# Moving VectorE sums of the last batch between small products, and sums of T1 beside the last product of batch 1

## The chip, the cores and the metric

One core of a Trainium2 chip. The metric is the device time of one execution in microseconds (us). The span in a profile is the time from its first to its last instruction; in these runs it is about 2 us shorter than the time. Only one core runs. TensorE is PE in the views, VectorE is DVE, ScalarE is ACT.

## The reference

```python
# x: 8 batches x 8 heads x 512 x 64, state: 8 x 8 x 32 x 64
a = softmax(scale * x @ state.T);   xread = a @ state       # 512 rows a batch
a2 = softmax(scale * state @ x.T);  sread = a2 @ x          # 32 rows a batch
y = concat(xread, sread)  ->  (8 * 544, 512)                # heads side by side
h = y @ w_in               # 512 x 2048
g = h * sigmoid(1.702 * h)
out = g @ w_out            # 2048 x 512
```

## The kernel before

All is fp32. From batch 1 on, the last product (g @ w_out) of a batch is done in Strassen's way, which needs seven block products in place of eight and some sums besides. They are called P1 to P7, in the order P1, P2, P5, P6, P3, P7, P4. P1, P2 and P3 are plain: 16 matmuls with an output of 128x256, each of which stands as two records in these traces (48 records of L706 for the 24 matmuls of P1's second half and P2 in the last batch). P5, P6, P7 and P4 are split once more into seven small products of 128x128 each. In batch 1, P5 and P4 are still plain. After batch 7, the last one, a final part takes the 256 rows of sread ("sr"), with sums of w_in that VectorE has to have ready by then. T1 to T4 are sums of blocks of w_out.

TensorE does the products; VectorE forms the sums that go into them and adds the results out of PSUM, the buffer (in banks) that the matmuls of this kernel write to. A sum that nobody needs soon can stand in the program in front of an add for which TensorE waits, and in these traces VectorE ran them in the program's order: in the last batch before, TensorE's last record of P2 ended at 644.76 us, but the add that reads P2's bank started at 650.98, behind the eight half sums ahead of it. `hook("P5.4")` means: what is listed under this name is put here, after the fourth small product of P5.

```python
        product(bank(0), A_of(0, 0), B11, "P1")      # hooks "P1a", "P1b" after its two halves
        nc.scalar.copy(k1, bank(0))
        sums_of(S2, q1, q2, q4)
        if not plain:
            ...
            sums_of(S1, *r)
            third_of(S1)
        product(bank(1), A_of(0, 1), B21, "P2")      # hooks "P2a", "P2b"
        osb = opool.tile([P, 2, HN], FP32, tag="osb", name=f"osb_{key}_00")
        tt(osb, bank(1), k1)                         # reads P2's PSUM bank
        ...
            o, h0, h1 = low_banks()                  # o is bank 1 once more
            strassen_low(left_of(S1, *r), (b11, t3, b21, b22, *low5), [h0, h1, o], p5, at)   # P5

    def strassen_low(left, right, bank, R, at):      # cut to its first products
        product(o[0], a11, b11); nc.scalar.copy(p, o[0]);  at(1)
        product(o[1], s2, t2);   add(u2, o[1], p);         at(2)
        product(o[2], a12, b21); add(c11, o[2], p);        at(3)   # o[2] is P2's bank
        product(o[0], a21, t3);  add(u3, o[0], u2);        at(4)
        ...
```

For the last batch the twenty half sums of w_in (`steps`) are handed out like this:

```python
            order = [("P1b", 2), ("P2a", 8)]
            order += [(name, 1) for name in ("P5.4", "P5.6", "P6.1", ..., "P7.4")]
```

And in batch 1 the three sums of T1 are made at the hook S4, just ahead of P6, into spare buffers, and stored to DRAM:

```python
    def low5_make():
        rooms = spare_M()
        for fn, args in low_sums(T1, [v.rearrange("p (f n) -> p f n", f=QF) for v in rooms[:3]]):
            fn(*args)
        for k in range(3):
            nc.sync.dma_start(outside[5][:, FC * k : FC * (k + 1)], rooms[k])
```

Of the kernel before, what the change touches and what calls it, by code (L numbers as in the profile page):

```python
# [20 lines left out]
def kernel(  # L21
# [30 lines left out]
    nc = tc.nc  # L52

    B, H, S, D = x.shape
# [9 lines left out]
    FC = 512  # L64
# [37 lines left out]
    T1, T2, T4 = (sums[:, i].rearrange("p (f n) -> p f n", f=HF) for i in range(3))  # L102
# [25 lines left out]
    def load_state(b):  # L128
        stn[b] = apool.tile([P, NG, D], FP32, tag="stn", name=f"stn_{b}", bufs=2)
        for g in range(NG):  # L130
            nc.sync.dma_start(stn[b][:, g], st_v[b, g])
# [44 lines left out]
    for i, v in enumerate((8.0 * most, 8.0 * (most - least))):  # L176
        t = konst.tile([P, 1], FP32, name=f"edge_{i}")
# [332 lines left out]
    def quarters(key, u, ntok):  # L510

        g, half = G[key, u], ntok // 2
        return g[:, :, :half], g[:, :, half:ntok]

    def s12(key, u, ntok):

        half = ntok // 2
        (a11, a21), (_, a22) = quarters(key, u, ntok), quarters(key, HF // 2 + u, ntok)
        s1, s2 = S1[:, 2 * u : 2 * u + 2, :half], S2[:, 2 * u : 2 * u + 2, :half]
        nc.vector.tensor_tensor(out=s1, in0=a21, in1=a22, op=ALU.add)  # L520
        nc.vector.tensor_tensor(out=s2, in0=s1, in1=a11, op=ALU.subtract)

    def s3(key, u, ntok):

        a11, a21 = quarters(key, u, ntok)
        nc.vector.tensor_tensor(out=a21, in0=a11, in1=a21, op=ALU.subtract)
# [61 lines left out]
    QF = HF // 2  # L588
    T3 = w_out[:, :HF, HN:]
# [4 lines left out]
    low5 = low3  # L594
    outside = {k: dram.tile([P, 3 * FC], FP32, name=f"low_{k}") for k in (3, 4, 5)}
    turn_room = low[:, 3:].rearrange("p k n -> p (k n)")

    def low_load(k):
        nc.sync.dma_start(turn_room, outside[k])
# [21 lines left out]
    def spare_M():  # L621

        m = [mpool.tile([P, NG, FC], FP32, tag=f"M{i}", name="spare_M") for i in (2, 3)]
        return [v[:, g] for v in m for g in range(NG)]

    def low5_make():
        rooms = spare_M()
        for fn, args in low_sums(T1, [v.rearrange("p (f n) -> p f n", f=QF) for v in rooms[:3]]):
            fn(*args)
        for k in range(3):  # L630
            nc.sync.dma_start(outside[5][:, FC * k : FC * (k + 1)], rooms[k])

    def halves_of(t):

        return [t[:, QF * i : QF * (i + 1), P * k : P * (k + 1)] for i in range(2) for k in range(2)]

    def low_sums(t, rooms):

        b11, b12, b21, b22 = halves_of(t)
        t1, t2, t4 = rooms  # L640
        return [(T_of, v) for v in ((t1, b12, b11), (t2, b22, t1), (t4, b21, t2))]

    def low_third(t):
        _, b12, _, b22 = halves_of(t)
        T_of(b12, b22, b12)
# [39 lines left out]
    def strassen_two(key, dst, hooks, a4):  # L685


        plain = a4 is None
# [7 lines left out]
        def hook(name):  # L696
            for fn, args in hooks.get(name, ()):
                fn(*args)
# [121 lines left out]
        b11, t3, b21, b22 = halves_of(T3)  # L820
        o, h0, h1 = low_banks()
        strassen_low(left3, (b11, t3, b21, b22, *low3), [h0, h1, o], k3, lambda i: hook(f"P7.{i}"))
        if key + 1 < B:
            low_load(5)
        hook("P7")
        osb = opool.tile([P, 2, HN], FP32, tag="osb", name=f"osb_{key}_11")
# [118 lines left out]
    def parts_x(b):  # L945

        a = A[b]
        t1, t2, t3, t4 = ([t] for t in a["T"])
        r11, r21, r22 = [a["aT"][:, 0, :QT]], [a["aT"][:, 1, :QT]], [a["aT"][:, 1, QT:]]

        def left(u):
            c = u // 2
            lo, hi = a["M", c], a["M", 2 + c]
            return [lo[:, 0]], [lo[:, 1]], [hi[:, 0]], [hi[:, 1]], [a["S1"][:, c]], [a["S2"][:, c]], [a["S4"][:, c]]

        return left, (r11, r21, r22, t1, t2, t3, t4)
# [40 lines left out]
    def up_strassen(b, ntok, left, right):  # L997

        QT = ntok // 2
        b11, b21, b22, t1, t2, t3, t4 = right  # L1000
        banks = {}

        def product(u, bank, lhs, rhs, first):
            if first:
                if bank == "x":
                    banks[bank, u] = psH.tile([P, 2, QT], FP32, tag="h", name=f"upx_{b}_{u}")
                else:
                    o = bank_o[2 * (u % 2) + (bank == "z")]
                    banks[bank, u] = o[:, : 2 * QT].rearrange("p (k t) -> p k t", k=2)
            ps = banks[bank, u]  # L1010
            n = len(lhs)
            for k in range(2):
                o = 2 * P * (u % 2) + P * k
                for i in range(n):
                    nc.tensor.matmul(  # L1015
                        ps[:, k], lhs[i][:, o : o + P], rhs[i],
                        start=(first and k == 0 and i == 0), stop=(i == n - 1), skip_group_check=True,
                    )
            return ps

        def gelu(dst, src):
            nc.scalar.activation(out=dst, in_=src, func=AF.Gelu_apprx_sigmoid)  # L1022

        def add(ps, x, dst):
            nc.vector.tensor_tensor(out=dst, in0=ps, in1=x, op=ALU.add)  # L1025


        def begin(u):
            l11, l12, l21, l22, m1, m2, m4 = left(u)
            G[b, u], G[b, NU + u] = free.pop(0), free.pop(0)  # L1030
            _, c12 = quarters(b, u, ntok)
            c21, _ = quarters(b, NU + u, ntok)
            nc.scalar.copy(c21, product(u, "x", l11, b11, True))  # L1033
            add(product(u, "y", m2, t2, True), c21, c12)

        def middle(u):
            l11, l12, l21, l22, m1, m2, m4 = left(u)
            c11, c12 = quarters(b, u, ntok)
            c21, c22 = quarters(b, NU + u, ntok)
            z = product(u, "z", m1, t1, True)  # L1040
            gelu(c11, product(u, "x", l12, b21, False))
            add(product(u, "y", l21, t3, False), c21, c22)
            add(z, c22, c22)
            gelu(c22, c22)

        def end(u):
            l11, l12, l21, l22, m1, m2, m4 = left(u)
            c11, c12 = quarters(b, u, ntok)
            c21, c22 = quarters(b, NU + u, ntok)
            add(product(u, "y", l22, t4, False), c21, c21)  # L1050
            gelu(c21, c21)
            add(product(u, "z", m4, b22, False), c12, c12)
            gelu(c12, c12)
            if u:
                s12(b, u - 1, ntok)

        for u in range(NU):
            begin(u)
            if u:
                end(u - 1)  # L1060
            middle(u)

        def rest():
            end(NU - 1)
            s12(b, NU - 1, ntok)
            for u in range(NU):
                s3(b, u, ntok)

        return rest
# [86 lines left out]
    def T_of(t, x0, x1):  # L1156
        nc.vector.tensor_tensor(out=t, in0=x0, in1=x1, op=ALU.subtract)
# [34 lines left out]
    def out_of(b):  # L1192
        return lambda r, n: out_x[b, r, :, n].rearrange("r q n -> q r n")

    for b in range(1, B):
        if b > 1:
            ahead = {"P1a": [(up_strassen(b, S, *parts_x(b)), ())]}
        else:
            ahead = {
                "P1a": low_sums(T2, low2) + [(T_of, (T4, B21, T2)), (low_third, (T2,))],  # L1200
                "P1b": low_sums(T3, low3) + [(low_keep, (3, turn_room)), (low_third, (T3,))],
                "S4": [(low5_make, ())],
                "P7.5": [(low_third, (T1,))],
            }
        if b + 1 < B:
            hooks = hooks_next(b + 1)
        else:

            steps, left, right = sr_sums()
            order = [("P1b", 2), ("P2a", 8)]  # L1210
            order += [(name, 1) for name in ("P5.4", "P5.6", "P6.1", "P6.3", "P6.4", "P6.6", "P7.1", "P7.2", "P7.3", "P7.4")]
            hooks = {}
            for name, n in order:
                hooks[name], steps = steps[:n], steps[n:]
            assert not steps
            for name, t in (("P6.2", T1), ("P6", T2), ("P4.1", T3), ("P4.7", T4)):
                hooks[name] = [(low_third, (t,))]
        for name, first in ahead.items():
            hooks[name] = first + hooks.get(name, [])
        a4 = {}  # L1220
        k = 3 if b + 1 < B else 0
        hooks.setdefault("P3a", [])[k:k] = [(low4_load if b > 1 else low4_make, (a4,))]
        strassen_two(b, out_of(b), hooks, a4 if b > 1 else None)
        if b == 1:
            low_third(T4)
        if b + 2 < B:
            load_state(b + 2)
            load_x(b + 2)
# [35 lines left out]
```

## Time and profile before

| what | value |
|---|---|
| time | 741.96 us, median of three runs, 741.14 to 742.05 |
| the one execution with a profile | 740.57 us, span 738.7 us |
| TensorE busy | 97% of the span |
| its longest two waits | 5.2 us in the last batch, 1.6 us in batch 1 |
| one batch in the middle | 78.8 us |

The prediction shows the lines of the two waits. Two more readings carry its sums. The first is batch 6, where nothing stands in front of osb, in the timeline of the kernel before (start, us, engine, line, operation, count):

```profile
570.57 1.05 PE L656 MATMUL low<-sums,later 128*128 128x128 f32 x8
...
571.55 0.68 DVE L713 TENSOR_TENSOR osb<-o,g 128x512 f32<-128x512 f32 x1
...
572.36 1.09 PE L656 MATMUL o<-sums,later 128*128 128x128 f32 x8
...
576.85 1.06 PE L656 MATMUL low<-sums,later 128*128 128x128 f32 x8
```

The first and the last of these are the first small products of P5 and of P6: 6.28 us apart, with osb done before the third product is due. The second reading is free time of VectorE in the last batch, during the first half of P1:

```profile
633.58 0.69 DVE L1025 TENSOR_TENSOR g<-o,g 128x512 f32<-128x512 f32 x1 [2.90 <-PE o L1015]
```

VectorE stood idle for 2.90 us there until TensorE released it.

### The profile page before, as it was taken

What the parts mean: (1) busy time and instruction counts of PE and PEld (TensorE: products, weight loads), DVE (VectorE), ACT (ScalarE), POOL (GpSimd) and SP (SyncE); (2) the same over time, 40 slices, a digit from 0 to 9 for tenths busy, and PEclk for the clock granted to TensorE, in tenths of its full rate; (3) what the DMA queues carried; (4) which work ended last, traced back from release to release, by engine and by line L of the source; (5) the groups of instructions that cost most, each with busy time, mean ns of one, the idle gap of its engine ahead of it and who ended that gap; (6) DMA issues with size and microseconds to landing.
All of it is one profiled execution on the core that took longest, in us unless ns stands there. A gap on an engine that the chain in (4) does not pass through costs nothing.

```text
span 738.7 us, 11929 instructions
## 1 busy us (share of the span) xinstructions
PE 719.8 (97%) x4903; PEld 570.6 (77%) x4903; DVE 566.5 (77%) x1156; ACT 235.5 (32%) x436; POOL 0.8 (0%) x8
## 2 busy tenths in 40 slices
PE   8999999999999999999999999999999999979996
PEld 3333444477888889879888889888987898879995
DVE  6997999739866997689867985799669976788440
ACT  4786411033224511432144323442245114200220
POOL 0000000000000000000000000000000000000000
PEclk9999999999999999999999999999999999999999
DMA  9821244011150022201330115002400220020000
GB/s 235 341 96 48 99 158 118 0 58 69 75 146 1 13 88 91 57 1 58 114 76 1 58 47 144 1 17 85 136 12 1 77 108 3 1 101 30 15 1 28
DMA packets 52086, 51.88 MB, mean 70 GB/s; under 512 B 36800, under 2 KB 44480, under 8 KB 52032
## 3 DMA queue, kind: packets, MB, share of 16 engines
q1 hardware_dynamic: 52032, 51.13, 22.2%
q8 instruction: 38, 0.62, 0.3%
q14 instruction: 16, 0.13, 0.1%
HBM read 39.85 MB, written 11.27 MB: 69 GB/s over the span
## 4 chain that ended last, share of the span: by engine, by line
PE 90%; DVE 5%; ACT 2%; DMA 2%; issue 1%; SPq 0%; DVEq 0%; ACTq 0%
PE o L706 19%; PE o L1015 16%; PE low L656 14%; PE o L497 7%; PE o L656 7%; PE h L479 7%; PE upx L1015 6%; PE M L303 4%; PE o L540 2%; PE xT L282 2%; PE o L303 1%; PE sr L459 1%; PE warm L123 1%; PE upx_sr L1015 1%; DMA out_dram<-osb_sr 1%; DVE g L713 1%
## 5 line engine op out<-in xcount | busy, mean ns | idle before, releaser
L1025 DVE TENSOR_TENSOR g<-o,g 128x512 f32<-128x512 f32 (+1 forms) x140 | 88.1, 650 | 85.4 <-PE o L1015 84.5
L706 PE MATMUL o<-w_out,g 128*128 128x256 f32 x672 | 152.7, 381 | 0.0
L706 PEld LDWEIGHTS o<-w_out,g 128*128 128x128 f32 x672 | 125.2, 190 | 26.2 <-issue 10.5
L1022 ACT ACTIVATE g<-g 128x512 f32<-128x512 f32 (+1 forms) x84 | 49.8, 599 | 100.5 <-DVE g L1025 100.5
L1015 PE MATMUL upx<-aT,M 128*128 128x256 f32 x192 | 49.3, 379 | 0.0
L1015 PE MATMUL o<-ta,M 128*128 128x256 f32 x192 | 49.3, 379 | 0.0
L1015 PE MATMUL o<-ta,ms 128*128 128x256 f32 x192 | 48.3, 379 | 0.0
L439 ACT COPY M<-M 128x512 f32<-128x512 f32 x64 | 33.2, 596 | 37.7 <-PE M L303 37.7
L1015 PEld LDWEIGHTS o<-ta,M 128*128 128x128 f32 x192 | 36.5, 190 | 5.0
L1015 PEld LDWEIGHTS o<-ta,ms 128*128 128x128 f32 x192 | 36.5, 190 | 5.0
L1015 PEld LDWEIGHTS upx<-aT,M 128*128 128x128 f32 x192 | 36.1, 190 | 4.7
L656 PE MATMUL low<-sums,later 128*128 128x128 f32 x264 | 34.6, 279 | 0.0
L520 DVE TENSOR_TENSOR later<-g,g 128x512 f32<-128x512 f32 (+1 forms) x32 | 20.8, 649 | 17.6 <-ACT g L482 17.6
L656 PEld LDWEIGHTS low<-sums,later 128*128 128x128 f32 x264 | 33.0, 196 | 0.4
L303 PE MATMUL M<-w_in,stT 64*32 64x512 f32 x512 | 32.7, 594 | 0.2 <-ACT eT L449 0.2
L479 PE MATMUL h<-low,M 128*128 128x512 f32 x64 | 29.8, 600 | 1.4 <-DVE low L388 1.4
L479 PE MATMUL h<-aT,M 128*128 128x512 f32 x64 | 28.7, 599 | 1.4 <-ACT M L439 1.4
L497 PE MATMUL o<-w_out,g 128*128 128x512 f32 x64 | 28.7, 594 | 0.0
L497 PE MATMUL o<-w_out,sums 128*128 128x512 f32 x64 | 28.4, 594 | 0.0
L1033 ACT COPY g<-upx 128x512 f32<-128x512 f32 x24 | 13.7, 572 | 42.4 <-PE upx L1015 42.4
L482 ACT ACTIVATE g<-h 128x512 f32<-128x512 f32 x24 | 14.0, 592 | 40.5 <-PE h L479 40.5
L479 PEld LDWEIGHTS h<-aT,M 128*128 128x128 f32 x64 | 11.8, 190 | 18.3 <-issue 12.2
(200 smaller groups left out, 1262.8 us busy)
## 6 DMA issues: line engine op xcount, KB each, us to landing
low<-low SPq DMA_DIRECT2D x20, 768.0 KB
later<-in_moe_w_out_dram SPq DMA_DIRECT2D x16, 512.0 KB
xn<-in_x_dram SPq DMA_DIRECT2D x28, 256.0 KB
w_out<-in_moe_w_in_dram SPq DMA_DIRECT2D x12, 512.0 KB
out_dram<-osb SPq DMA_DIRECT2D x18, 256.0 KB
out_dram<-later SPq DMA_DIRECT2D x14, 256.0 KB
later<-in_moe_w_in_dram SPq DMA_DIRECT2D x4, 512.0 KB
sums<-in_x_dram SPq DMA_DIRECT2D x4, 256.0 KB
```

The source lines that it names most:

```text
L282: nc.tensor.transpose(ps[:, c], x_heads(b, c, j), ident)
L303: nc.tensor.matmul(ps[g][st], A[b]["stT"][rows, st], rhs(rows, j), start=True, stop=True)
L439: nc.scalar.copy(m[:, g], ps[g])
L479: nc.tensor.matmul(hps, lhs[i], rhs[i], start=(i == 0), stop=(i == n - 1))
L497: nc.tensor.matmul(ops, G[key, f // 2][:, f % 2, P * r : P * (r + 1)], w_out[:, f], start=(f == 0), stop=(f == NF - 1))
L520: nc.vector.tensor_tensor(out=s1, in0=a21, in1=a22, op=ALU.add)
L540: nc.tensor.matmul(ps[:, r], lhs[f][:, P * r : P * (r + 1)], rhs[:, f], start=(first and r == 0 and f == 0), stop=(f == HF - 1), skip_grou ...
L656: nc.tensor.matmul(ps, lhs[f], rhs[:, f], start=(f == 0), stop=(f == QF - 1))
L706: nc.tensor.matmul(ps[:, r], lhs[f][:, P * r : P * (r + 1)], rhs[:, f], start=(r == 0 and f == 0), stop=(f == HF - 1), skip_group_check=True,)
L1015: nc.tensor.matmul(ps[:, k], lhs[i][:, o : o + P], rhs[i], start=(first and k == 0 and i == 0), stop=(i == n - 1), skip_group_check=True,)
L1022: nc.scalar.activation(out=dst, in_=src, func=AF.Gelu_apprx_sigmoid)
L1025: nc.vector.tensor_tensor(out=dst, in0=ps, in1=x, op=ALU.add)
```

## The change

Its intent is to take both waits from TensorE by giving VectorE the same sums in another order. In the last batch four half sums go to the idle time in P1, the other sixteen one by one (twice two small ones together) between small products (one of them beside P3), and none stays between P1 and osb. In batch 1 the sums of T1 move beside the plain P4, and go straight to the buffer where batch 2 reads them. Cut to its core:

```diff
-    def low5_make():
-        ...
-        if key + 1 < B:
+        if not plain and key + 1 < B:
             low_load(5)
@@ batches
+            if b == 2:
+                ahead["P7.5"] = [(low_third, (T4,))]
...
-                "S4": [(low5_make, ())],
-                "P7.5": [(low_third, (T1,))],
+                "P4.7": low_sums(T1, low5) + [(low_keep, (5, turn_room)), (low_third, (T1,))],
@@ the last batch
-            order = [("P1b", 2), ("P2a", 8)]
-            order += [(name, 1) for name in ("P5.4", "P5.6", "P6.1", ..., "P7.4")]
-            ...
-            for name, t in (("P6.2", T1), ("P6", T2), ("P4.1", T3), ("P4.7", T4)):
-                hooks[name] = [(low_third, (t,))]
+            order = (
+                ("P5.4", 2), ("P5.6", 3), ("P6.1", 6), ("P6.3", 7), ("P6.4", 8), ("P6.6", 9), ("P3a", 10), ("P7.1", 11),
+                ("P7.2", 16, 17), ("P7.3", 18, 19), ("P7.4", 12), ("P7.6", 13), ("P4.4", 14), ("P4.6", 15),
+            )
+            hooks = {name: [steps[i] for i in n] for name, *n in order}
+            hooks["P6.2"] = [(low_third, (T1,))]
+            hooks["P4.7"] = [(low_third, (t,)) for t in (T2, T3, T4)]
+            ahead["P1a"][:0] = [steps[i] for i in (0, 1, 4, 5)]
...
-        if b == 1:
-            low_third(T4)
```

More of the change, by code (lines that the diff above doesn't have):

```diff
@@ L624, in spare_M @@
         return [v[:, g] for v in m for g in range(NG)]
-    def low5_make():
-        rooms = spare_M()
-        for fn, args in low_sums(T1, [v.rearrange("p (f n) -> p f n", f=QF) for v in rooms[:3]]):
-            fn(*args)
-        for k in range(3):
-            nc.sync.dma_start(outside[5][:, FC * k : FC * (k + 1)], rooms[k])
     def halves_of(t):
@@ L1209 @@
             steps, left, right = sr_sums()
-            order = [("P1b", 2), ("P2a", 8)]
-            order += [(name, 1) for name in ("P5.4", "P5.6", "P6.1", "P6.3", "P6.4", "P6.6", "P7.1", "P7.2", "P7.3", "P7.4")]
-            hooks = {}
-            for name, n in order:
-                hooks[name], steps = steps[:n], steps[n:]
-            assert not steps
-            for name, t in (("P6.2", T1), ("P6", T2), ("P4.1", T3), ("P4.7", T4)):
-                hooks[name] = [(low_third, (t,))]
+            order = (
[6 more added lines that the diff above has]
+            ahead["P1a"][:0] = [steps[i] for i in (0, 1, 4, 5)]
         for name, first in ahead.items():
```

## The prediction

> **What bounds the kernel now.** I read the page first, then the list of who waited for whom on TensorE, then the timeline around each wait, and last the same stretch of an undisturbed batch.
>
> ```profile
> span 738.7 us, 11929 instructions
> ...
> PE 719.8 (97%) x4903; PEld 570.6 (77%) x4903; DVE 566.5 (77%) x1156; ACT 235.5 (32%) x436; POOL 0.8 (0%) x8
> ...
> PE   8999999999999999999999999999999999979996
> ...
> DVE  6997999739866997689867985799669976788440
> ```
>
> TensorE (PE) is busy 97% of the span, so the end is set by PE's own work plus the few places where PE stands still. After the opening only the 36th slice is below 9, near 650 us, and the last ones. A slice is 18.5 us and hides short holes, so the list of waits comes next (releaser, us in total, times, longest).
>
> ```profile
> PE o L656 <- DVE osb L713: 5.2, 1, 5.2
> PE o L656 <- DVE pu L659: 1.6, 1, 1.6
> PE h L479 <- DVE low L388: 1.4, 1, 1.4
> ```
>
> The two longest happen once each, both in L656 (the small 128x128 products), both for VectorE (DVE). The third lies in the opening, which the change leaves alone. The timeline places the 5.2 us in the last batch, inside P5, between its second and third small product (start, us, engine, line, what, count, idle before):
>
> ```profile
> 645.49 1.06 PE L656 MATMUL low<-low,spare_M 128*128 128x128 f32 x8
> ...
> 646.16 1.28 DVE L975 TENSOR_TENSOR ws<-ws,w_in 128x512 f32<-128x512 f32 x2
> 647.37 1.28 DVE L975 TENSOR_TENSOR w_in<-w_in,w_in 128x512 f32<-128x512 f32 x2
> 648.57 1.28 DVE L975 TENSOR_TENSOR ws<-w_in,ws 128x512 f32<-128x512 f32 x2
> 649.77 1.28 DVE L975 TENSOR_TENSOR ws<-w_in 128x512 f32<-128x512 f32 x2
> 650.98 0.68 DVE L713 TENSOR_TENSOR osb<-o,g 128x512 f32<-128x512 f32 x1
> ...
> 651.71 1.98 PE L656 MATMUL o<-sums,later 128*128 128x128 f32 x8 [5.17 <-DVE osb L713]
> ```
>
> The third product writes the PSUM bank that P2 filled, and that bank is free only when DVE has read it (osb). In DVE's order eight half sums of w_in (L975) stand in front. And after the hole that product took 1.98 us where its neighbours take 1.06. In batch 1 the same picture is smaller: three sums of T1 (spare_M, L1157) and a row sum stand ahead of the add (pu) that frees a bank.
>
> ```profile
> 182.58 0.68 DVE L1157 TENSOR_TENSOR spare_M<-sums 128x512 f32<-128x512 f32 x1
> ...
> 183.30 1.42 DVE L1157 TENSOR_TENSOR spare_M<-sums,spare_M 128x512 f32<-128x512 f32 x2
> 184.63 0.68 DVE L410 TENSOR_REDUCE sm<-e 128x16 f32<-128x512 f32 x1
> 185.23 0.28 DVE L659 TENSOR_TENSOR pu<-o,pu 128x128 f32<-128x128 f32 x1
> ...
> 185.56 1.16 PE L656 MATMUL o<-low,g 128*128 128x128 f32 x8 [1.60 <-DVE pu L659]
> ```
>
> [...]in the window 651.7 to 655.2 us, just after the 5.17 us hole, the granted clock is 0.52, and in 180.2 to 185.5 us, around the 1.60 us hole, it is 1.00. So the first hole costs more than its length and the second does not. [...] The trace shows PE starting at 651.71, 0.05 us after osb ended at 651.66.[...]
>
> **The change part by part.** All durations are rows of the trace before. A 128x512 sum of DVE lasts 0.68 us, but the next starts 0.60 us after it where it doesn't depend on it; one that depends starts 0.72 after.
>
> (1) Last batch, P1 to P2. Ten half sums leave this stretch (two after the quarter sums, eight ahead of osb), some 10 x 0.60 = 6.0 us. Four go to the first half of P1, ahead of the rest of the up product. There DVE is idle 2.90 us (630.68 to 633.58, waiting for PE); four take 4 x 0.60 plus 0.08 for the one that depends, about 2.5 us, so they end near 633.2 and delay nothing. Then the chain runs as before but two sums (1.2 us) shorter: the last sum ahead of osb, which ended at 646.24, ends at 645.0; P2 is done on PE near 644.8 (its last product starts its successor at 644.60). So osb runs 645.0 to 645.7. The third product of P5 is due at 644.60 + 2 x 0.89 = 646.38. The margin is 0.7 us, and PE doesn't wait.
>
> What that is worth: P5's first product to P6's first took 644.60 to 657.91 = 13.31 us. The same stretch of batch 6, with no hole, took 570.57 to 576.85 = 6.28 us. Saved: 7.0 us, of which 5.2 us are the hole and the rest (1.8) the slow clock after it: products three and four took 1.78 and 1.71 us from start to start in place of 0.89 each.
>
> (2) Where the six others of those ten and the rest go: one half sum after a small product. A product takes PE 0.89 us; DVE needs 0.20 for the add and 0.60 for the sum, 0.80, as the old P6 already shows with no wait of PE. The densest is P7: two sums ahead of its first add, then two pairs of 128x256 sums (0.34 each), then two more. From the second product to the fourth DVE needs about 0.2 + 0.7 per 0.89 us. PE looks at a bank again three products later, so a lag of some tenths is covered. Cost: 0.
>
> (3) End of P4: three "third" sums (T2, T3, T4) now stand together ahead of the last sum and of the first add of the final up product; before it was one. That is 2 x 0.60 = 1.2 us later. That add began at 685.63 after 0.37 us of idle DVE, so it moves by about 0.8 us and ends near 686.85. PE comes back to its bank with a weight load at 687.04. It fits by 0.2 us; if not, it costs some tenths.
>
> (4) Batch 1. The three sums of T1 (2.05 us of DVE) leave the place ahead of P6. The add that frees the bank then ends near 183.45; its product is due at 180.23 + 4 x 0.89 = 183.80. The wait is gone. From P6's first product to the transposes it took 180.23 to 188.34 = 8.11 us, in batch 6 576.85 to 583.10 = 6.25. Saved: 1.86, call it 1.8 us. The sums come back with the third of T1 beside P4, where DVE is idle 3.36 us (209.34 to 212.70) and saves another 0.60 since the third of T1 leaves P7: 4 sums with two dependent steps are 2.7 us, so they fit.
>
> (5) T4's third moves from the front of the up product of batch 2 to its P7 (0.60 us in a slot of 0.89). A DRAM read of 768 KB goes away, and three writes become one. DMA bounds nothing here (its queue holds 22% of the span). Cost and gain: 0.
>
> Sum: 7.0 + 1.8 = 8.8 us, so 741.96 - 8.8 = 733.2 us.
>
> **The rivals.** (a) A new wait replaces the old: osb is freed, and PE then stops at P5's later products, P7, or the first up product of the last part, because the half sums crowd there. For it: margins of 0.2 to 0.7 us, and P7's DVE load. Against it: bank reuse is three products away, and batches 2 to 6 carry similar loads with no wait in the list. If P5 stopped for 1 to 2 us, the time would be 734.5 to 735.5.
> (b) The hole shrinks but stays, because the four sums in P1 must wait for a buffer and push the chain: say they start only at 632. Then the chain is about 1.3 us later than I say, and osb ends near 647.0, 0.6 us too late. [...]nearly all is gained: about 734.
> (c) The slow clock of PE was not due to the hole, and only 5.2 + 1.6 = 6.8 us come back: 735.2. The window with 0.52 speaks against it.
> (d) The freed DVE time hides nothing and DVE sets the pace: then 742. DVE's idle time in the last batch and PE's 97% speak against it.
>
> **Range and chances.** The middle is 733.2; 0.5 us of scatter either way (the runs before spread over 0.9), and the rivals all lie above. So 731.8 to 735.6. Faster by over 2% needs below 727.4, nearly 6 us more than all the waits I found; slower would need a wait of 15 us. I give 0.01 and 0.01.
>
> **What would show it right or wrong.** In the new list of waits both L656 entries are gone, and the 0.52 window with them; P5's first product to P6's first is 6.3 us in the last batch; P6's stretch of batch 1 is 6.25; osb of the last batch ends before the second product of P5 does; the batches between keep their 78.8 us (371.17 to 450.00 between two of them). It is wrong if PE's total idle time falls by less than 6 us, if a new wait above 0.5 us stands at P5, P7 or the final up product, or if the 78.8 us change.

## The result, and the profile after

| | time, median | all runs | span profiled |
|---|---|---|---|
| before | 742.0 us | 741.14 to 742.13 (4 runs) | 738.7 |
| after | 731.5 us | 731.45 to 731.81 (4 runs) | 729.7 |

The ratio is 0.9862 (95% interval 0.9845 to 0.9879). The kernel is faster by 1.4%, within the 2% that I gave 0.98. But 731.5 lies 1.7 us below the predicted 733.2 and 0.3 below my range. In this table the times differ by 10.5 us and the profiled spans by only 9.0.

The changed file is seven lines shorter ahead of these places, so L656 is L649 here, L713 is L706, L975 is L968, L1015 is L1008 and L1025 is L1018. From the page of the changed kernel:

```profile
PE 716.4 (98%) x4901; PEld 568.6 (78%) x4903; DVE 566.8 (78%) x1156; ACT 235.4 (32%) x436; POOL 0.8 (0%) x8
...
PE   7999999999999999999999999999999999999996
```

The hollow slice near 650 us is gone. TensorE's waits, longest first:

```profile
PE h L479 <- DVE low L388: 1.5, 1, 1.5
PE h L479 <- ACT M L439: 1.4, 2, 0.8
PE stT L272 <- DMA stn<-in_state_dram: 1.3, 1, 1.3
```

No wait of the small products is left; what is on top now belongs to the opening. The last batch in the timeline:

```profile
628.87 1.28 DVE L968 TENSOR_TENSOR ws<-w_in 128x512 f32<-128x512 f32 x2
...
630.07 1.29 DVE L968 TENSOR_TENSOR w_in<-w_in,w_in 128x512 f32<-128x512 f32 x2
...
631.86 0.69 DVE L1018 TENSOR_TENSOR g<-o,g 128x512 f32<-128x512 f32 x1 [0.50 <-PE o L1008]
...
642.88 1.05 PE L649 MATMUL low<-sums,later 128*128 128x128 f32 x8
643.24 0.68 DVE L706 TENSOR_TENSOR osb<-o,g 128x512 f32<-128x512 f32 x1
...
644.66 1.06 PE L649 MATMUL o<-sums,later 128*128 128x128 f32 x8
...
649.13 1.06 PE L649 MATMUL low<-sums,later 128*128 128x128 f32 x8
```

The four half sums fill the idle time (0.50 us of it is left), osb ends at 643.92, the third product starts at 644.66 without waiting, and P5's first product to P6's first takes 649.13 - 642.88 = 6.25 us. Batch 1:

```profile
183.25 0.28 DVE L652 TENSOR_TENSOR pu<-o,pu 128x128 f32<-128x128 f32 x1
...
183.87 1.06 PE L649 MATMUL o<-low,g 128*128 128x128 f32 x8
...
186.55 1.04 PE L448 MATMUL eT<-ident,e 128*128 128x128 f32 x8
```

P6 began at 180.30, so 6.25 us to the transposes. In this pair of traces the two stretches are as the prediction worked them out (9.0 us between the spans, 8.8 predicted). I looked for the missing 1.5 us in executions that I hadn't seen.

Two of the prediction's other signs: the batches between keep their length (78.84 us between the same products, 78.83 before). TensorE's idle time, span less busy time, falls from 18.9 to 13.3 us, 5.6 and so less than the 6 that the prediction asked for. But this trace has a wait of 1.3 us for a DMA in the opening that the one before lacks; a second trace of the changed kernel (a7 below), without that wait, has 11.9 us, a fall of 7.0.

### The profile page after: what moved, and what is told of

Its sections match the earlier page's. It is cut to its first block, busy times and chain, and to the rows that moved or that the text cites. A ratio compares the mean times of both kernels' runs of the same rounds, so it can differ in the third digit from the quotient of the medians.

```text
span 729.7 us, 11916 instructions
## 1 busy us (share of the span) xinstructions
PE 716.4 (98%) x4901; PEld 568.6 (78%) x4903; DVE 566.8 (78%) x1156; ACT 235.4 (32%) x436; POOL 0.8 (0%) x8
## 4 chain that ended last, share of the span: by engine, by line
PE 95%; ACT 2%; DMA 2%; SPq 0%; DVE 0%; issue 0%; DVEq 0%; ACTq 0%
PE o L699 22%; PE o L1008 17%; PE low L649 15%; PE o L497 8%; PE o L649 7%; PE h L479 7%; PE upx L1008 6%; PE M L303 4%; PE o L540 2%; PE xT L282 2%; PE o L303 1%; PE sr L459 1%; PE warm L123 1%; PE upx_sr L1008 1%; DMA out_dram<-osb_sr 1%; PE eT L448 1%
## 5 line engine op out<-in xcount | busy, mean ns | idle before, releaser
L1018 DVE TENSOR_TENSOR g<-o,g 128x512 f32<-128x512 f32 (+1 forms) x140 | 88.1, 651 | 82.4 <-PE o L1008 81.5
L699 PEld LDWEIGHTS o<-w_out,g 128*128 128x128 f32 x672 | 125.2, 190 | 26.2 <-issue 10.5
L1015 ACT ACTIVATE g<-g 128x512 f32<-128x512 f32 (+1 forms) x84 | 49.8, 600 | 100.5 <-DVE g L1018 100.5
L1008 PE MATMUL upx<-aT,M 128*128 128x256 f32 x192 | 49.3, 379 | 0.0
L1008 PE MATMUL o<-ta,M 128*128 128x256 f32 x192 | 49.3, 379 | 0.0
L1008 PE MATMUL o<-ta,ms 128*128 128x256 f32 x192 | 48.3, 379 | 0.0
L1008 PEld LDWEIGHTS o<-ta,M 128*128 128x128 f32 x192 | 36.5, 190 | 5.0
L1008 PEld LDWEIGHTS o<-ta,ms 128*128 128x128 f32 x192 | 36.5, 190 | 5.0
L1008 PEld LDWEIGHTS upx<-aT,M 128*128 128x128 f32 x192 | 36.1, 190 | 4.7
L649 PE MATMUL low<-sums,later 128*128 128x128 f32 x264 | 33.7, 275 | 0.0
L649 PEld LDWEIGHTS low<-sums,later 128*128 128x128 f32 x264 | 32.1, 192 | 0.4
```

Source lines behind the costliest of these rows:

```text
L649: nc.tensor.matmul(ps, lhs[f], rhs[:, f], start=(f == 0), stop=(f == QF - 1))
L699: nc.tensor.matmul(ps[:, r], lhs[f][:, P * r : P * (r + 1)], rhs[:, f], start=(r == 0 and f == 0), stop=(f == HF - 1), skip_group_check=True,)
L1008: nc.tensor.matmul(ps[:, k], lhs[i][:, o : o + P], rhs[i], start=(first and k == 0 and i == 0), stop=(i == n - 1), skip_group_check=True,)
L1015: nc.scalar.activation(out=dst, in_=src, func=AF.Gelu_apprx_sigmoid)
L1018: nc.vector.tensor_tensor(out=dst, in0=ps, in1=x, op=ALU.add)
```

## The experiments

Theory A: after the 5.2 us hole TensorE runs at half clock for a while (0.52 granted from 651.7 to 655.2 us in the trace before), and for how long differs from one execution to the next. The one that I had profiled was a cheap one. Theory B: the profiled execution was short for another reason, in the opening or at the end.

**The kernel before again (no edit).**

> The kernel before, unchanged, run again with a profile. Theory A (the slow clock after the 5.2 us hole costs more in most executions than in the one I had profiled): spans of most runs near 740.1, over the 738.7 profiled; mean granted clock of those runs near 0.995 in place of 0.997; if the new profile falls on such a run, the half-clock window after the hole lasts 5 to 7 us and not 3.5, and P5's first product to P6's first takes 14.5 to 15 us in place of 13.3. Theory B (the profiled run was short for a reason elsewhere, in the opening or the end): spans near 740.1 too, but the clock 0.997 in all and P5 to P6 13.3 us.

Five runs of it took 740.39 to 742.11 us, and nine of the control, the same kernel, 740.67 to 742.14. Span and mean granted clock go together: all runs with spans of 738.5 to 738.8 have a clock of 0.996 or 0.997, those of 739.2 to 740.0 have 0.995, and those of 740.1 have 0.993. That is theory A's pattern. (One later control run, on another chip, has 740.1 with 0.995.) The stored trace was that of a short run (738.5), with 13.04 us for the stretch, so it didn't show the long case.

**Two more looks at the kernel before (no edit).**

> The kernel before once more, one look for its trace. Theory A has so far traces of executions with spans of 738.5 and 738.7 only, where the slow clock cost 1.4 to 1.8 us. If this one has a span of 739.2 or more: P5's first product to P6's first takes 13.9 us or more and the extra lies in the products just after the hole, all else as before. If the stretch is 13.0 to 13.4 in such a trace, theory A is wrong and the extra is elsewhere.

> The same again, since about two in five executions are short ones: the span less the stretch from P5's first product to P6's first of the last batch is 725.3 within 0.3 us in every trace (738.7 less 13.3 is 725.4), whatever the span.

The first was short again (740.52 us). The second was a long one, 741.65 us. Its timeline after the hole:

```profile
651.78 2.08 PE L656 MATMUL o<-sums,later 128*128 128x128 f32 x8 [5.17 <-DVE osb L713]
653.65 1.91 PE L656 MATMUL low<-sums,later 128*128 128x128 f32 x8
655.36 1.87 PE L656 MATMUL low<-low,spare_M 128*128 128x128 f32 x8
657.06 1.06 PE L656 MATMUL o<-low,later 128*128 128x128 f32 x8
```

Three small products are slow here, where the trace behind the prediction has two. The same stretch of time in both traces, first the execution of the prediction, then this one (from:to, length, busy time and count of five engines, granted clock, DMA share, GB/s):

```profile
651.70:657.10 5.40, 5.39 (x33) 5.39 (x34) 3.62 (x9) 0.00 (x0) 0.00 (x0) 0.68 0.14 49
```

```profile
651.70:657.10 5.40, 5.32 (x25) 5.32 (x26) 3.20 (x8) 0.00 (x0) 0.00 (x0) 0.50 0.15 49
```

The clock stands at 0.50 throughout in the long one. Taking the stretch out leaves nothing to explain:

| execution of the kernel before | span | P5's first to P6's first | span less stretch |
|---|---|---|---|
| behind the prediction | 738.7 | 13.31 | 725.4 |
| a1_before_again | 738.5 | 13.04 | 725.5 |
| d1_before_look | 738.6 | 13.07 | 725.5 |
| d2_before_look | 739.6 | 14.19 | 725.4 |

The rest of the kernel is the same within 0.1 us, so theory B falls. In these four the slow clock cost 1.5 to 2.6 us: the stretch less 6.25 of work and less 5.32 of hole (the start of the third product less that of the first, 7.11, less 1.79). Runs of 740.1 come to 3.1 by the same sum, an estimate from their span.

**The last batch alone.** The kernel before with the diff's part "the last batch" only.

> The last batch's part of the change alone, batch 1 as before. Theory A: 733.3 us (the 10.5 us measured less 1.8 for batch 1), clock 0.998 or more in every run. Theory B: 735.0 (7.0 us less), the clock as in A. The hole of 1.6 us in batch 1 stays.

Measured 733.81 us, 733.58 to 733.88, clock 0.999 in all. That is 7.4 us less than its control's median of 741.25. It agrees with neither number well: 0.5 over A's, 1.2 under B's. A's 733.3 is the changed kernel's 731.5 plus 1.8 for batch 1, so batch 1's part is worth more than 1.8: here 2.3, and 2.1 between the spans (731.8 and 729.7). In the traces 1.86 us of it stand in P6's stretch of batch 1. Another 0.2 us come at the very end: from the start of TensorE's last record to the end of the span it takes 5.9 us in the four traces of kernels that have batch 1's part and the old end (after, a3, a7, c1), and 6.1 in the eight without that part. Why is not known. The scatter is small: 0.3 us in place of the control's 1.5, since the hole is gone.

**Batch 1 alone.** The same, the other way round.

> Batch 1's part of the change alone, the last batch as before. Theory A: 740.2 us (1.8 us less), the hole of 5.2 us and a half-clock window after it as in the kernel before, whose length may differ. Theory B: the missing 1.5 us came from here or from the opening: 738.5 to 738.8.

Measured 739.09 us, 738.49 to 739.87, clock 0.993 to 0.997: 2.2 us less, and the scatter stays with the hole. The median is nearer to B's number (738.5 to 738.8) than to A's 740.2, but both were counted from 742.0. Counted from the control of the same rounds (741.25), A's would be 739.4 and B's about 737.9. From the traces: span less stretch is 725.4 before and 729.7 - 6.25 = 723.45 after, so batch 1's part is worth 1.9 to 2.0 in this pair, with the opening and the end.

**TensorE kept busy in the hole.** One line in the kernel before's last batch:

```diff
+            def filler(n):
+                ps = att_ps([P, P], "filler")
+                for _ in range(n):
+                    nc.tensor.matmul(ps, ident, ident, start=True, stop=True)
+
+            hooks["P5.2"] = [(filler, (44,))]
```

> The kernel before with 44 small products of the identity by itself, into a free bank, put on TensorE inside the hole: the wait for osb stays, but TensorE isn't idle in it. The half-clock window goes (clock 0.999). Theory A: 742.0 less 3.3 = 738.7 us. Theory B: 742.0 less 1.8 = 740.2 us. A third theory, that the slow products after the hole have nothing to do with its being idle: 742.0, unchanged.

Measured 743.59 us: slower, and neither theory's number. The trace shows my mistake: 44 products are 88 records of 0.11 us, 9.8 us in a hole of 5.2. Even so the run tells something: five runs within 0.3 us, clock 0.998 or 0.999. So I ran it with 22.

> The filler of the run before was twice as long as planned ([...]9.8 us in a hole of 5.2). With half of it, 4.9 us, it fits inside the hole. Theory A (slow clock after the hole, 1.4 to 3.4 us depending on the execution): the hole stays, every run is within 0.2 us of the others, clock 0.998 or more, span near 737.0, so 739.0 us: below every run of the kernel before, by 1.5 against its best and 3.1 against its worst. If the slow products had another cause than idleness: 740.4 to 742.1, as scattered as before.

Measured 739.31 us, 739.16 to 739.38, clock 0.998 or 0.999; 739.0 was expected. The nine control runs took 740.55 to 742.17, each above each of these.

```profile
646.80 5.08 PE L1222 MATMUL filler<-ident 128*128 128x128 f32 x44
...
652.14 1.16 PE L656 MATMUL o<-sums,later 128*128 128x128 f32 x8 [0.26 <-DVE osb L713]
653.14 1.06 PE L656 MATMUL low<-sums,later 128*128 128x128 f32 x8
```

The third product still starts after osb, 6.23 us after the second as before, but it and the next run at full speed (clock 1.00 from 645 to 657 us). So here it was being idle that slowed the clock (0.993 to 0.997 in the control's runs, 0.998 or 0.999 with the filler), and that costs 2.2 us between the medians (741.53 - 739.31), 1.2 to 2.9 between this median and the fastest and slowest of the control.

**A shorter hole.** The kernel before with four half sums in P1 and six ahead of osb:

```diff
-            order = [("P1b", 2), ("P2a", 8)]
+            order = [("P2a", 2, 3, 6, 7, 8, 9)]
...
+            ahead["P1a"][:0] = [steps[i] for i in (0, 1, 4, 5)]
```

> The kernel before with four half sums in P1's idle time as in the change, and six (in place of eight) left ahead of osb: the hole shrinks from 5.2 to about 2.9 us[...]. Theory A[...]: no half-clock window, runs within 0.2 us, clock 0.998, span near 739.3 less 2.3 less 2.7 (what the slow clock costs on average), so 734.7 to 735.0 and 736.7 us. If the clock cost went with the length of the hole: 1.2 us of it would stay, near 737.9, and the runs scatter by about 1.

Measured 738.5, 738.47, 738.31, 738.59 and 736.97 us. My expectation, that the clock holds over a hole of this length, was an estimate that no trace had shown. It came true in the fifth run alone (clock 0.999, span 734.9); in the other four the clock was 0.997 and the span 736.4 or 736.5. The trace is one of those four:

```profile
649.48 2.04 PE L656 MATMUL o<-sums,later 128*128 128x128 f32 x8 [2.77 <-DVE osb L713]
651.31 1.85 PE L656 MATMUL low<-sums,later 128*128 128x128 f32 x8
653.00 1.06 PE L656 MATMUL low<-low,spare_M 128*128 128x128 f32 x8
```

A hole of 2.77 us cost 1.5 us of span in four executions of five over what it cost in the fifth; in the trace it made two slow products. So in single executions the cost is not in proportion to the hole: 1.5 to 2.6 us after 5.17 us in the traces before. With the edges of the view put where the clock changes, it gives, for the execution of the prediction, for the long one, and for this run:

```profile
648.42:651.84 3.42, 0.13 (x1) 0.13 (x2) 3.42 (x7) 0.00 (x0) 0.00 (x0) 1.00 0.00 0
651.84:655.25 3.41, 3.41 (x17) 3.41 (x18) 2.11 (x5) 0.00 (x0) 0.00 (x0) 0.50 0.23 77
655.25:658.66 3.41, 3.41 (x32) 3.41 (x32) 2.82 (x8) 0.00 (x0) 0.00 (x0) 1.00 0.10 27
```

```profile
646.81:650.22 3.41, 0.00 (x0) 0.00 (x0) 3.41 (x7) 0.00 (x0) 0.00 (x0) 1.00 0.00 0
650.22:653.64 3.42, 1.86 (x8) 1.86 (x9) 2.90 (x6) 0.00 (x0) 0.00 (x0) 0.50 0.23 77
653.64:657.05 3.41, 3.41 (x18) 3.41 (x17) 1.78 (x4) 0.00 (x0) 0.00 (x0) 0.50 0.00 0
657.05:660.46 3.41, 3.41 (x33) 3.41 (x32) 2.79 (x8) 0.27 (x1) 0.00 (x0) 1.00 0.31 94
```

```profile
646.14:649.55 3.41, 0.64 (x7) 0.45 (x5) 3.41 (x7) 0.00 (x0) 0.00 (x0) 1.00 0.00 0
649.56:652.97 3.41, 3.41 (x16) 3.41 (x17) 2.15 (x5) 0.00 (x0) 0.00 (x0) 0.50 0.23 77
```

The first numbers after the length are TensorE's busy time; the clock is the third from the end. After the hole the clock is at 0.50 for 3.41 us in the prediction's trace and in a5, and for 6.83 us in d2. In a1 the mean clocks (0.95 over 645 to 652 us, 0.83 over 652 to 660) give about 3.4 us, from 651.3 to 654.7, an estimate. For d1 and a3 the starts of the products tell: from the third to the fifth it takes 3.26 us in d1, 1.79 at full clock; from the third to the sixth 4.66 us in a3, 2.68 at full clock. That is 1.5 and 2.0 us more.

The times between changes of the clock on record are 645.12, 3.41 and 81.92 us in the prediction's trace and 723.63 us in the changed kernel's: 189, 1, 24 and 212 times 3.413 us. The first stretch at full clock on record begins 6.72 us into the span in the one and 3.87 in the other.

In the 3.41 us before the fall TensorE was busy for 0.13 us (the prediction's trace), 0.00 (d2) and 0.64 (a5), so it was not always idle from end to end. From 645.01 to 648.42 us in the prediction's trace it was busy for 1.53 us, and the clock was 1.00 then and in the 3.42 us that followed. In d2 it was busy for 1.86 us in the first 3.42 us at half clock, and the clock stayed at 0.50 for 3.41 us more. It came back after 3.41 us of which TensorE was busy for all (the prediction's trace, d2, a5) or, in a1, for about 2.85.

The cost in each of these traces is half of the half-clock time in which TensorE has work: (655.25 - 651.84) / 2 = 1.7 us for the prediction's execution, (654.71 - 651.86) / 2 = 1.4 for a1, (657.05 - 651.78) / 2 = 2.6 for d2; for d1 the starts give 1.5. The sums above gave 1.7, 1.5, 2.6 and 1.5. The hole is 5.17 us in all four, so its length alone doesn't decide how long the clock stays low. That it depends on where the hole falls between steps of 3.41 us, which lie differently over the kernel in each execution, fits these figures; it is my estimate, and no run tested it. Of the fifth run of this experiment no trace was kept. A hole of 2.77 us that is split between two such steps could leave TensorE busy for over 1.53 us in both, which would fit, an estimate too and not shown.

**The margin at the end of P4.** The changed kernel with three more sums behind the three that the change put there:

```diff
+            def extra():
+                for v in spare_M()[:3]:
+                    T_of(v.rearrange("p (f n) -> p f n", f=2), T1[:, :2], T1[:, 2:4])
+
+            hooks["P4.7"] += [(extra, ())]
```

> The changed kernel with three more sums of 128x512 (into a spare buffer) behind the three at the end of P4, to test the margin of 0.2 us that my third step gave. If the step is right: the first add of the final up product ends 1.8 us later, PE waits about 1.6 us for it, 733.1 us. If there was more room than I thought, below 732.

Measured 733.35 us, span 731.3 in place of 729.7. The changed kernel itself has, at that place, the add from 677.61 to 678.03 and the next product on its bank at 678.37:

```profile
677.61 0.42 DVE L1018 TENSOR_TENSOR g<-o,g 128x256 f32<-128x256 f32 x1
...
678.37 1.06 PE L1008 MATMUL o<-ta_sr,w_in 128*128 128x128 f32 x8
```

With three more sums:

```profile
679.40 0.42 DVE L1018 TENSOR_TENSOR g<-o,g 128x256 f32<-128x256 f32 x1
679.88 1.16 PE L1008 MATMUL o<-ta_sr,w_in 128*128 128x128 f32 x8 [1.36 <-DVE g L1018]
```

The add came 1.79 us later and the product 1.51 later, so the margin was 0.3 us: the third step of the prediction was right, and nearly at its limit.

**A version below both.** The changed kernel with two more buffers for the four stores at the end:

```diff
-            o = opool.tile([P, nb, HN], FP32, tag="osb", name=f"osb_{key}_{i}{k}")
+            tag = {(0, 0): None, (1, 1): "M2", (1, 0): "M3", (0, 1): None}[i, k]
+            if tag:
+                o = mpool.tile([P, NG, FC], FP32, tag=tag, name=f"osb_{key}_{i}{k}")[:, 0, : nb * HN]
+                o = o.rearrange("p (r n) -> p r n", r=nb)
+            else:
+                o = opool.tile([P, nb, HN], FP32, tag="osb", name=f"osb_{key}_{i}{k}")
```

> A try to go below both: the changed kernel with two more output buffers for the four stores at the end, where two of the last sums wait 3.4 us for the DMA of the store before. PE ends first and the last sum then starts 0.8 us earlier: 0.8 us less than the changed kernel, 730.7 us. If that DMA is slowed by the one it now overlaps: 731.5, unchanged.

Measured 730.97 us, 730.86 to 731.06; 730.7 was expected. The last sum of the changed kernel, then of this one:

```profile
725.08 0.42 DVE L559 TENSOR_TENSOR osb_sr<-o,g 128x256 f32<-128x256 f32 x1 [3.44 <-DMA out_dram<-osb_sr]
```

```profile
724.35 0.42 DVE L564 TENSOR_TENSOR osb_sr<-o,g 128x256 f32<-128x256 f32 x1 [3.03 <-PE o L540]
```

It waits for TensorE now, not for the store before. This and the changed kernel I then ran on one chip:

> The changed kernel as it is, for a comparison on one chip with more runs: 731.5 within 0.3 in every run, clock 0.998 or more. Against a mean of the kernel before near 741.3 (23 runs so far), a ratio of 0.9868, so 9.8 us and not the 10.5 of the first four runs.

> The version with two more output buffers on the same chip as the changed kernel: its last sum started 0.7 us earlier in the trace, so 730.8 to 731.0 against 731.5, below it in every run.

The changed kernel took 731.44 us (731.40 to 731.48), ratio to before 0.9866 (0.9851 to 0.9881); the version with more buffers 730.89 us (730.74 to 731.01), ratio 0.9859. Each of its runs is below each of the changed kernel's: 0.55 us, less than one part in a thousand, but real. The runs of the kernel before on that chip have a median of 741.23 us, so the change is worth 9.8 us, and not the 10.5 of the first four, of which three fell on long executions.

## Why the prediction was right and wrong

*Step 1, the last batch.* The mechanism was right: the four sums fit the idle time, osb ended 0.74 us before the third product (0.7 predicted), and the stretch took 6.25 us (6.28 predicted). The term that failed is "the rest (1.8) the slow clock after it". I read it in one execution and took it for a constant. It costs about 1.5 to 3.1 us by execution (the upper end is an estimate), 2.2 between medians: after the same hole the clock was low for 3.41 us in one execution and for 6.83 in another. And I subtracted it from 741.96, a median of executions of 741.14 to 742.05, while the trace was of one with 740.57. From 740.57 the same sum of 8.8 gives 731.8; 731.5 was measured. For an execution near 742.0 the slow clock is about 3.1 (the estimate above for spans of 740.1, which runs of 742.1 have), so the same steps give 741.96 - 5.3 - 3.1 - 1.9 = 731.7. The remaining 0.2 is about what the end of the kernel became shorter, which no step had. The table before had the hint: 740.57 lay below all three runs.

*Step 2, one half sum after each small product:* right; no wait of TensorE in P5, P6, P7 or P4.

*Step 3, the crowded end of P4:* right; margin 0.3 us measured, 0.2 predicted.

*Step 4, batch 1:* right; 8.11 us became 6.25. The kernel with this alone was 2.2 us faster, between the traces it is 1.9 to 2.1, of which 0.2 stand at the end of the kernel; the prediction had 1.8.

*Step 5, T4 and the DMA:* no cost seen; the 0.2 us at the end came with batch 1's part, and which of its edits brings them was not tested.

*The rivals.* (a), (b) and (d) didn't happen. (c), that the slow clock was not due to the hole, was wrong, as the filler shows (739.31 us, clock 0.998 or 0.999). All four lay above 733.2, so the range had 1.4 us below its middle and 2.4 above, and the scatter that I allowed for (0.5 either way) was smaller than the 1.8 us over which 31 executions of the kernel before spread (740.39 to 742.17). The prediction took every doubt to be on the slow side. Two of its sums are off and change nothing: 2% below 741.96 is 727.1, not 727.4, and (a)'s 1 to 2 us on top of 733.2 are 734.2 to 735.2.

What stays open: what decides how long the clock stays low, how little work of TensorE makes it fall and how much brings it back, what the fifth run of the shorter hole looked like, and the 0.2 us at the end.

## What to carry to other kernels

When an engine's wait leaves TensorE idle for a few microseconds, look in the trace for slow products after it and count them too (here there were some after holes of 5.17 and 2.77 us, and none after the 1.60 us of batch 1, where the clock was 1.00). Take that cost as a range: here it was 1.5 to 2.6 us for one and the same hole in four executions. Start from the time of the execution whose trace the terms come from, not from a median of others. And when an engine is not the bound but one of its adds frees a bank, give it its less urgent work in the gaps after that add: here the same sums in another order were worth 9.8 us.
